# Every SBUF addition and subtraction on VectorE, new durations in the planner, and q/k copies that read runs

## The chip, the cores and the metric

The kernel runs on one core of one Trainium2 chip. The metric is the device time of one launch in microseconds (us), taken as the median of several runs. Five engines work side by side, each through its own list of instructions in order: TensorE (PE, matmuls; PEld is its weight load), VectorE (DVE), ScalarE (ACT), GpSimd (POOL), and SyncE (SP), which here issues all DMAs.

## The reference

Attention with two paths is followed by two feed-forward blocks, all in float32, with batch 4, 8 heads, 576 positions and head dimension 64.

```
# "down" path: q, k, v averaged over 4 neighbours, full softmax attention over 144 positions, repeated 4 times
out_up    = repeat(softmax(q_d @ k_d.T / 8) @ v_d, 4)
# local path: each position sees positions less than 4 away
out_local = softmax(where(|i-j| < 4, q @ k.T / 8, -1e9)) @ v
x = (out_up + out_local) as (2304 tokens, 512)
h = (x @ w1) * (x @ w2) @ w3;  y = h @ w_out            # block A, 1024 wide
z = max(y @ m1, y @ m2, y @ m3);  out = z @ m_out       # block B, 768 wide
```

The feed-forward weights are float64 words in memory and are turned into float32 on the chip.

## The kernel before

**The pieces of work.** `down(b, hp)` does the averaged path for one batch and one pair of heads; there are 16 of them. It loads q and k for the pair as one tile `qk`, copies q and k into position order with two ScalarE copies (L392), folds `qk` twice by additions (L397, L399), makes the scores on PE (L408), the exponentials on ScalarE (L423), scales them (L432), transposes them on PE, folds v twice (L447, L449) and multiplies (L456). `slab(n, ...)` does the local path of 192 tokens of a batch; there are 12. A slab needs the q and k planes and the `down` results of all four head pairs of its batch. Two slabs make the input `xt` of one chunk of 384 tokens.

**The weights.** `weights_product` multiplies w3 by w_out on PE (L591) after `float32` has turned their words into floats: one ScalarE instruction (L358) and four on VectorE (L359, L360, L362, L364) for each tile of 128x1024. The tiles are called `wf`. `pair` does the same for each two blocks of the other weights (tile `cv`) and then splits them: eight pairs for block A, twelve for block B, which can only be loaded into the places that block A has left.

**The split.** All matmuls of the blocks take their operands as a high and a low half: `split` rounds on ScalarE (L334) and subtracts (L336) to get the low half. `mm3` (L341 to L343) is three matmuls for each product. A unit of block A or B is `front` (matmuls `pf`, then `z` by L618 and L620, then a split into `g`) and two units later `back` (matmuls `py`). Block A has 6 chunks of 8 units, block B 6 chunks of 6.

**The order.** Nothing is run in the order in which it is written. `Program.add` notes each task with its engine, its duration in us as a formula of its size, what it reads and what it writes. `Program.order` works out from that a start for each task: `forward` plays the program on a model in which each engine does one task at a time, and takes the ready task with the earliest due time; `backward` works out the due times again; of six rounds the shortest is kept. The engines then run the tasks in exactly that order, whatever the real times are. PE's matmul groups of the blocks are chained in the order of the units; all other tasks move freely.

A task with several options is put by `forward` on the engine that would end it first (L238 to L246). The options are those of `either`: VectorE at 0.18 + 0.00115 us per element, or GpSimd at 0.2 + 0.0024. They are used for L397, L399, L432, L447, L449 and for the subtraction of `split` when its source is in SBUF (L336 for `w`, `xt`, `yt`, `g`). In the trace before, 94 of these run on GpSimd. The model knows of no influence of one engine on another. A task on one engine that feeds another on the same engine counts no delay between them (`lag`); with several options, or from engine to engine, it counts 0.12 to 0.30 us.

Of the kernel before, what the change touches and what calls it, by code (L numbers as in the profile page):

```python
# [15 lines left out]
B, H, S, D = 4, 8, 576, 64  # L16
P = 128
HP = H // 2
NB2 = 2
NR = B // NB2  # L20
NC = 16
TC = S // NC
TT = 12
NJ = TC // TT
NCH = NR * NJ
TG = 4
NG = TT // TG
# [5 lines left out]
GD = S // TG  # L33
# [34 lines left out]
def view(ap, offset, dims):  # L68

    return bass.AP(ap.tensor, ap.offset + offset, [ap.ap[0]] + dims)  # L70
# [202 lines left out]
def attention_moe_kernel(ctx, tc, q0, k0, v0, mask0, ql, kl, vl, mask, qkp, vp, w12, w3t, wo, m123, mo, out):  # L273
# [4 lines left out]
    prog = Program()  # L278
# [23 lines left out]
        return Tile(others, [P, 512], F32, name)  # L302


    act = lambda n: [("ACT", 0.19 + n * 0.00085)]
    dve = lambda n: [("DVE", 0.16 + n * 0.00104)]
    psum = lambda n: [("DVE", 0.15 + n * 0.00104)]
    quick = lambda n: [("DVE", 0.12 + n * 0.0006)]
    either = lambda n: [("DVE", 0.18 + n * 0.00115), ("POOL", 0.2 + n * 0.0024)]
    pe = lambda us: [("PE", us)]  # L310

    def dma(dst, src, reads, writes, size):
# [66 lines left out]
    planes, ods = {}, {}  # L379

    def down(b, hp):
        rd, i = b // NB2, b % NB2 * HP + hp
        qk, k, w = tqr.tile([P, TG * 2 * GD], F32, "qk"), kr.tile([P, KEYS], F32, "k"), qr.tile([P, QUERIES], F32, "q")
        planes[b, hp] = w, k
        dma(lambda: qk(), lambda: qkp[rd, i], [], [qk], P * S * 8)
        v = vrr.tile([KH, 2, 4 * P], F32, "vr")
        dma(lambda: v(), lambda: vp[rd, i].rearrange("r p n -> p r n"), [], [v], KH * 4096 * 2)
        prog.add([("POOL", 0.12)], lambda e: e.memset(k()[:, :W], 0.0), [], [(k, 1)])
        prog.add([("POOL", 0.12)], lambda e: e.memset(k()[:, W + S:], 0.0), [], [(k, 2)])
        prog.add([("POOL", 0.12)], lambda e: e.memset(w()[:, S:], 0.0), [], [(w, 1)])  # L390
        for to, x in ((lambda: w()[:, :S], 0), (lambda: k()[:, W:W + S], GD)):
            prog.add(act(S), lambda e, to=to, x=x: e.copy(  # L392
                to().rearrange("p (c g r) -> p c g r", c=NC, r=TG), view(qk(), x, [[1, NC], [NC, NJ * NG], [2 * GD, TG]])),
                [qk], [(k if x else w, 0)])

        s, vd = qk, vdr.tile([KH, 2, P], F32, "vd")
        prog.add(either(4 * GD), lambda e: e.tensor_tensor(  # L397
            qk()[:, :4 * GD], qk()[:, :4 * GD], qk()[:, 4 * GD:], op=ALU.add), [], [qk])
        prog.add(either(2 * GD), lambda e: e.tensor_tensor(  # L399
            s()[:, :2 * GD], qk()[:, :2 * GD], qk()[:, 2 * GD:4 * GD], op=ALU.add), [], [s])  # L400

        sp = bank("sp")

        def scores(e):
            for w in range(QT):
                for a in range(2):
                    h = slice(a * D, (a + 1) * D)
                    e.matmul(  # L408
                        sp()[h, w * GD:(w + 1) * GD], s()[h, w * QS:w * QS + D], s()[h, GD:2 * GD],
                        start=True, stop=True,  # L410
                    )


        ex = er.tile([P, QT, GD], F32, "e")
        prog.add(pe(0.9), scores, [s], [sp, ex])
        two = twor.tile([P, 2, QT], F32, "two")
        spv = lambda: sp()[:, :QT * GD].rearrange("p (t n) -> p t n", t=QT)
        prog.add(psum(QT * GD), lambda e: e.reduce_max(two()[:, 0], spv(), axis=AX.X), [sp], [two])
        prog.add(act(3), lambda e: e.mul(two()[:, 0], two()[:, 0], -SCALE / 16.0), [], [two])

        def exponentials(e):
            for w in range(QT):
                e.activation(  # L423
                    ex()[:, w, :], spv()[:, w, :], AF.Exp, bias=two()[:, 0, w:w + 1], scale=SCALE / 16.0,
                    accum_out=two()[:, 1, w:w + 1],
                )

        prog.add([("ACT", 1.75)], exponentials, [sp], [ex, two])
        prog.add([("POOL", 0.25)], lambda e: e.tensor_scalar(
            two()[:, 1], two()[:, 1], 4.0, 4e-9, op0=ALU.mult, op1=ALU.add), [], [two])  # L430
        prog.add([("DVE", 0.17)], lambda e: e.reciprocal(two()[:, 1], two()[:, 1]), [], [two])
        prog.add(either(QT * GD), lambda e: e.tensor_tensor(  # L432
            ex(), ex(), view(two(), QT, [[1, QT], [0, GD]]), op=ALU.mult), [two], [ex])
        pt = dpr.tile([KH, 2, 2, QT, QW], F32, "dp")
        for part in range(2):
            pp = bank("pp")

            def transposed(e, part=part, pp=pp):
                for w in range(QT):
                    e.transpose(pp()[:KH, w * P:(w + 1) * P], ex()[:, w, part * KH:(part + 1) * KH], ident)  # L440

            prog.add(pe(0.4), transposed, [ex], [pp, (pt, part)])
            prog.add(act(288), lambda e, part=part, pp=pp: e.copy(
                pt()[:, part].rearrange("p a t n -> p t a n"),
                view(pp()[:KH, :], 0, [[P + QW - QS, QT], [D, 2], [1, QW]]),
            ), [pp], [(pt, part)])
        prog.add(either(4 * P), lambda e: e.tensor_tensor(  # L447
            v()[:, 0], v()[:, 0], v()[:, 1], op=ALU.add), [], [v])
        prog.add(either(2 * P), lambda e: e.tensor_tensor(  # L449
            vd().rearrange("p h n -> p (h n)"), v()[:, 0, :2 * P], v()[:, 0, 2 * P:], op=ALU.add), [v], [vd])  # L450
        po = bank("po")

        def values(e):
            for a in range(2):
                for k in range(2):
                    e.matmul(  # L456
                        po()[a * D:(a + 1) * D, :GD], vd()[:, k, a * D:(a + 1) * D],
                        pt()[:, k, a].rearrange("p t n -> p (t n)"), start=(k == 0), stop=(k == 1),
                    )

        if hp == 0:
            ods[b] = odr.tile([P, HP, GD], F32, "od")
        od = ods[b]
        prog.add(pe(0.7), values, [vd, pt], [po, (od, hp)])
        prog.add(act(GD), lambda e: e.copy(
            od()[:, hp].rearrange("p (c g) -> p c g", c=NC), view(po(), 0, [[1, NC], [NC, NJ * NG]])), [po], [(od, hp)])


    def slab(n, xt, at):
        b, s = divmod(n, NSL)  # L470
# [19 lines left out]
        st = sr.tile([P, 2, 2, HP, BK], F32, "s")  # L490
        sps = [bank("sq") for _ in range(2)]
# [11 lines left out]
                            q[h, t:t + 32], k[h, t:t + BK], start=True, stop=True,  # L503
                        )

        prog.add(pe(2.4), scores, [x for hp in range(HP) for x in planes[b, hp]], [*sps, st])
        for a in range(2):
            prog.add(psum(256), lambda e, a=a: e.tensor_tensor(
                view(st(), a * 256, [[P, 2], [BK, HP], [1, BK]]), view(sps[a](), 0, [[P, 2], [BK, HP], [1, BK]]),
# [53 lines left out]
    def weights_product():  # L563
        raw_places = [place[i] for i in (8, 9, 10, 11, 6, 7)]
        kept = {}

        def plain(at, h, srcs):

            raw = words(raw_places[plain.n % len(raw_places)], srcs, "raw")
            plain.n += 1  # L570
            if h == 0:
                kept[at] = Tile(place[at], [P, 2, 1024], F32, "wf")
            both = kept[at]
            float32(raw, (both, h), lambda: both()[:, h])
            return [((both, h), lambda i=i: both()[:, h, i * 512:(i + 1) * 512]) for i in range(2)]

        plain.n = 0
        wos, w3s = [], [[], []]
        for i in range(NF // 2):
            wos += plain(i // 2, i % 2, [wo[2 * i], wo[2 * i + 1]])  # L580
            w3s[0] += plain(2 + i // 2, i % 2, [w3t[2 * i, :, 0], w3t[2 * i + 1, :, 0]])
        for i in range(NF // 2):
            w3s[1] += plain(4 + i // 2, i % 2, [w3t[2 * i, :, 1], w3t[2 * i + 1, :, 1]])
        for half in range(2):
            os = [Tile(b, [P, 512], F32, "pw") for b in acc]
            for n in range(NF):
                (dw, w), (do, o) = w3s[half][n], wos[n]

                def product(e, n=n, w=w, o=o, os=os):
                    for i in range(4):  # L590
                        e.matmul(os[i](), w()[:, i * P:(i + 1) * P], o(), start=n == 0, stop=n == NF - 1)  # L591

                prog.add(pe(3.5), product, [dw, do], os, chained=True)
            for i in range(4):
                if i % 2 == 0:
                    wp = Tile(place[8 + half * 2 + i // 2], [P, 2, 2, 512], F32R, "wp")
                split(lambda i=i, wp=wp: wp()[:, i % 2, 0], lambda i=i, wp=wp: wp()[:, i % 2, 1], os[i], 512, [os[i]], wp,
                      from_psum=True)
                wa[half * 4 + i, 2] = wp, lambda i=i, wp=wp: wp()[:, i % 2]
# [101 lines left out]
    for n in range(len(units) + LAG):  # L701
# [17 lines left out]
        while gone and gone[0][0] <= n:  # L719
            _, p, f, i = gone.pop(0)  # L720
# [108 lines left out]
```

## Time and profile before

| | |
|---|---|
| median of 3 runs | 828.25 us (823.25 to 828.64) |
| the profiled execution | 827.7 us, span 825.9 us, mean granted PE clock 0.975 |
| PE busy | 771.5 us, 93% of the span |
| DVE busy | 399.7 us, 48% |
| ACT busy | 274.9 us, 33% |
| POOL busy | 138.6 us, 17% |

The span is from the first to the last instruction; the launch adds 1.8 us in the profiled execution. A busy share is a mean over the whole span, so it has to be read for each stretch by itself. A group of instructions is given by its line, engine, operation and tiles, with its busy time and the mean duration of one; where a row gives three durations, they are the shortest, the median and the longest. The granted clock is the share of full speed that TensorE was given: 1.00 is its level of 2.4 GHz, 0.50 its level of 1.2 GHz.

### The profile page before, as it was taken

How to read it: one execution, taken by the hardware profiler on the slowest of the kernel's cores; microseconds unless marked ns; L12 is line 12 of the kernel's file. 1: busy time of each engine (PE TensorE's matmuls, PEld its weight loads, DVE VectorE, ACT ScalarE, POOL GpSimd, SP SyncE). 2: the span in 40 equal slices, each digit the busy share in tenths (PEclk: the TensorE clock that was granted, in tenths of full speed). 3: DMA queues.
4: the chain of work that ended last, by engine and by line, in shares of the span. 5: the costliest groups of instructions: out<-in, count | busy, mean ns of one | idle time of the engine just before them, and what ended most of it. 6: DMA issues, size and time to landing. Idle time of an engine off the chain costs nothing.

```text
span 825.9 us, 16670 instructions
## 1 busy us (share of the span) xinstructions
PE 771.5 (93%) x7120; PEld 711.2 (86%) x7120; DVE 399.7 (48%) x614; ACT 274.9 (33%) x585; POOL 138.6 (17%) x176
## 2 busy tenths in 40 slices
PE   2879877998999999999998999999999999999997
PEld 0334446998999989999998999899999999999997
DVE  5978999924143274254324599972222131311211
ACT  4255574331234443363212355422121121121111
POOL 2213479500001012010001026520000000000000
PEclk9999976999999999999999999999999999999999
DMA  9786553012103232221202377112101001010001
GB/s 336 230 309 202 160 176 77 15 49 60 39 4 77 67 103 56 77 72 26 60 6 89 121 240 252 61 44 87 39 1 39 1 1 39 1 39 0 20 20 39
DMA packets 45482, 68.85 MB, mean 83 GB/s; under 512 B 20640, under 2 KB 29856, under 8 KB 45408
## 3 DMA queue, kind: packets, MB, share of 16 engines
q1 hardware_dynamic: 45408, 67.79, 25.7%
q8 instruction: 56, 0.92, 0.5%
q14 instruction: 18, 0.15, 0.1%
HBM read 58.33 MB, written 9.44 MB: 82 GB/s over the span
## 4 chain that ended last, share of the span: by engine, by line
PE 75%; DVE 11%; DMA 7%; issue 4%; ACT 1%; POOL 1%; SPq 1%; ACTq 0%; POOLq 0%; DVEq 0%
PE pf L341 16%; PE pf L343 15%; PE pf L342 15%; PE py L341 7%; PE py L342 6%; PE py L343 6%; PE poq L543 3%; DVE cv L362 3%; DMA qk<-qkp 2%; PE pw L591 2%; DVE cv L364 2%; DMA vr<-vp 2%; PE sq L501 1%; DVE cv L360 1%; PE sp L408 1%
## 5 line engine op out<-in xcount | busy, mean ns | idle before, releaser
L620 DVE TENSOR_TENSOR z<-pf,z 128x384 f32<-128x384 f32 x120 | 66.7, 556 | 287.5 <-PE pf L343 287.2
L341 PE MATMUL pf<-yt,w 128*128 128x384 f32 x432 | 146.0, 338 | 1.4 <-DVE z L620 1.4
L343 PE MATMUL pf<-yt,w 128*128 128x384 f32 x432 | 145.9, 338 | 0.0
L342 PE MATMUL pf<-yt,w 128*128 128x384 f32 x432 | 145.9, 338 | 0.0
L341 PE MATMUL pf<-xt,w 128*128 128x384 f32 x384 | 134.3, 350 | 1.9 <-issue 1.1
L342 PE MATMUL pf<-xt,w 128*128 128x384 f32 x384 | 132.0, 344 | 2.1 <-POOL xt L336 2.1
L343 PE MATMUL pf<-xt,w 128*128 128x384 f32 x384 | 131.6, 343 | 0.0
L618 ACT COPY z<-pf 128x384 f32<-128x384 f32 x84 | 40.2, 479 | 168.2 <-PE pf L343 168.2
L334 ACT CAST g<-z 128x384 fp32r<-128x384 f32 x84 | 43.1, 513 | 149.4 <-DVE z L620 149.3
L591 PE MATMUL pw<-wf 128*128 128x512 f32 x128 | 66.1, 669 | 24.9 <-DVE wf L364 22.6
L341 PEld LDWEIGHTS pf<-yt,w 128*128 128x128 f32 x432 | 81.1, 188 | 2.0 <-issue 1.7
L342 PEld LDWEIGHTS pf<-yt,w 128*128 128x128 f32 x432 | 81.1, 188 | 0.0
L343 PEld LDWEIGHTS pf<-yt,w 128*128 128x128 f32 x432 | 81.1, 188 | 0.0
L341 PEld LDWEIGHTS pf<-xt,w 128*128 128x128 f32 x384 | 73.9, 192 | 4.7 <-issue 2.7
L591 PEld LDWEIGHTS pw<-wf 128*128 128x128 f32 x128 | 26.6, 216 | 57.8 <-issue 32.4
L342 PEld LDWEIGHTS pf<-xt,w 128*128 128x128 f32 x384 | 73.8, 192 | 2.6 <-POOL xt L336 2.6
L343 PEld LDWEIGHTS pf<-xt,w 128*128 128x128 f32 x384 | 73.7, 192 | 0.0
L341 PE MATMUL py<-g,wp 128*128 128x384 f32 x192 | 67.1, 350 | 0.4 <-ACT o L649 0.4
L342 PE MATMUL py<-g,wp 128*128 128x384 f32 x192 | 64.8, 338 | 2.1 <-issue 2.1
L343 PE MATMUL py<-g,wp 128*128 128x384 f32 x192 | 64.9, 338 | 0.0
L336 DVE TENSOR_TENSOR g<-z,g 128x384 fp32r<-128x384 f32 x72 | 42.2, 587 | 33.3 <-ACT g L334 33.0
L341 PE MATMUL py<-g,w 128*128 128x384 f32 x144 | 48.9, 340 | 1.9 <-ACT o L649 1.9
(90 smaller groups left out, 1118.2 us busy)
## 6 DMA issues: line engine op xcount, KB each, us to landing
qk<-qkp SPq DMA_DIRECT2D x16, 576.0 KB
raw<-m SPq DMA_DIRECT2D x18, 512.0 KB
raw<-w3t SPq DMA_DIRECT2D x16, 512.0 KB
raw<-w SPq DMA_DIRECT2D x16, 512.0 KB
vr<-vp SPq DMA_DIRECT2D x16, 288.0 KB
y_dram<-o SPq DMA_DIRECT2D x48, 96.0 KB
y<-y_dram SPq DMA_DIRECT2D x16, 288.0 KB
out<-o SPq DMA_DIRECT2D x24, 192.0 KB
```

What stands on the lines that cost most here:

```text
L334: prog.add(act(n), lambda e: e.copy(hi(), src()), reads, [(writes, ("hi", id(hi)))])
L336: psum(n) if from_psum else either(n), lambda e: e.tensor_tensor(lo(), src(), hi().bitcast(F32), op=ALU.subtract),
L341: nc.tensor.matmul(o, wlo, xhi, start=first, stop=False)
L342: nc.tensor.matmul(o, whi, xlo, start=False, stop=False)
L343: nc.tensor.matmul(o, whi, xhi, start=False, stop=last)
L360: prog.add(quick(1024), lambda e: e.tensor_scalar(u(), u(), 3, 0x3FFFFFF8, op0=ALU.logical_shift_left, op1=ALU.bitwise_and), [], [cv])
L362: prog.add(dve(1024), lambda e: e.scalar_tensor_tensor(u(), high(), 0xC0000000, u(), op0=ALU.bitwise_and, op1=ALU.bitwise_or), [raw], [cv])
L364: prog.add(dve(1024), lambda e: e.scalar_tensor_tensor(u(), low(), 29, u(), op0=ALU.logical_shift_right, op1=ALU.bitwise_or), [raw], [cv])
L543: e.matmul(pos[u]()[a * D:(a + 1) * D, i * BQ:(i + 1) * BQ], vw()[h, a, i], pt().rearrange("p a n -> p (a n)")[h, c:c + BQ], start=True, s ...
L591: e.matmul(os[i](), w()[:, i * P:(i + 1) * P], o(), start=n == 0, stop=n == NF - 1)
L618: prog.add(act(T), lambda e, pp=pp: e.copy(z(), pp()[:, :T]), [pp], [z])
L620: prog.add(psum(T), lambda e, pp=pp: e.tensor_tensor(z(), pp()[:, :T], z(), op=ALU.mult if kind == "A" else ALU.max), [pp], [z])
```

## The change

The option of GpSimd is gone: `either` is now the same formula as `dve`, so all its users run on VectorE, and their tasks have one option. The formulas of ScalarE, of `quick` and `psum`, and four durations of PE groups are replaced. The two copies of L392 do the same reordering with the loops in another order: before, the innermost loop read elements 288 apart and wrote neighbours; now it reads runs of 16 neighbours (144 of them in a row) and writes elements 36 apart; their planned duration is 1.0 us. What is computed is the same. Since the planner works from the durations, the order on every engine is worked out anew.

```
-    act = lambda n: [("ACT", 0.19 + n * 0.00085)]
+    act = lambda n: [("ACT", 0.14 + n * 0.00098)]
     dve = lambda n: [("DVE", 0.16 + n * 0.00104)]
-    psum = lambda n: [("DVE", 0.15 + n * 0.00104)]
-    quick = lambda n: [("DVE", 0.12 + n * 0.0006)]
-    either = lambda n: [("DVE", 0.18 + n * 0.00115), ("POOL", 0.2 + n * 0.0024)]
+    psum = dve
+    quick = lambda n: [("DVE", 0.16 + n * 0.00052)]
+    either = dve
...
         for to, x in ((lambda: w()[:, :S], 0), (lambda: k()[:, W:W + S], GD)):
-            prog.add(act(S), lambda e, to=to, x=x: e.copy(
-                to().rearrange("p (c g r) -> p c g r", c=NC, r=TG), view(qk(), x, [[1, NC], [NC, NJ * NG], [2 * GD, TG]])),
+            prog.add([("ACT", 1.0)], lambda e, to=to, x=x: e.copy(
+                to().rearrange("p (c g r) -> p r g c", c=NC, r=TG),
+                qk().rearrange("p (r x g c) -> p r x g c", r=TG, x=2, c=NC)[:, :, x // GD]),
                 [qk], [(k if x else w, 0)])
...
-        prog.add(pe(0.9), scores, [s], [sp, ex])
+        prog.add(pe(0.95), scores, [s], [sp, ex])
...
-            prog.add(pe(0.4), transposed, [ex], [pp, (pt, part)])
+            prog.add(pe(0.45), transposed, [ex], [pp, (pt, part)])
...
-        prog.add(pe(0.7), values, [vd, pt], [po, (od, hp)])
+        prog.add(pe(1.05), values, [vd, pt], [po, (od, hp)])
...
-        prog.add(pe(2.4), scores, [x for hp in range(HP) for x in planes[b, hp]], [*sps, st])
+        prog.add(pe(1.55), scores, [x for hp in range(HP) for x in planes[b, hp]], [*sps, st])
...
-                prog.add(pe(3.5), product, [dw, do], os, chained=True)
+                prog.add(pe(3.45), product, [dw, do], os, chained=True)
```

## Rows read from the trace of the kernel before

**Rows 1.** The page: busy time of each engine over the whole span

```profile
PE 771.5 (93%) x7120; PEld 711.2 (86%) x7120; DVE 399.7 (48%) x614; ACT 274.9 (33%) x585; POOL 138.6 (17%) x176
```

**Rows 2.** Busy time by stretch: length, then each engine's busy us, PE clock, DMA

```profile
8.00:162.00 154.00, 121.97 (x1216) 77.54 (x1217) 140.85 (x164) 77.85 (x146) 73.49 (x65) 0.89 0.58 190
162.00:450.00 288.00, 281.98 (x3710) 268.26 (x3709) 111.63 (x228) 98.03 (x230) 23.11 (x49) 0.99 0.20 56
450.00:550.00 100.00, 96.30 (x657) 94.51 (x656) 82.65 (x96) 46.23 (x87) 35.56 (x25) 1.00 0.45 149
```

**Rows 3.** What PE waited for: us in total, times, longest

```profile
PE pw L591 <- DVE wf L364: 22.6, 3, 16.2
```

**Rows 4.** Busy time by stretch, two stretches at the low clock

```profile
105.00:111.80 6.80, 5.64 (x17) 3.13 (x18) 6.70 (x10) 3.46 (x11) 3.13 (x3) 0.50 0.45 133
122.00:139.10 17.10, 10.38 (x215) 9.14 (x212) 16.93 (x18) 10.21 (x22) 15.94 (x11) 0.50 0.40 100
```

**Rows 5.** Groups on POOL from 8 to 162 us: busy us, mean ns, idle before

```profile
L336 POOL TENSOR_TENSOR w<-cv,w 128x512 fp32r<-128x512 f32 x9 | 15.9, 1774 | 1.8 <-ACT w L334 1.0 <-DVE two L431 0.7
L447 POOL TENSOR_TENSOR vr<-vr 72x512 f32<-72x512 f32 x8 | 12.5, 1568 | 6.7 <-DVE cv L360 3.7 <-DMA vr<-vp 2.8
L397 POOL TENSOR_TENSOR qk<-qk 128x576 f32<-128x576 f32 x7 | 11.5, 1649 | 16.1 <-ACT k L392 16.1
L449 POOL TENSOR_TENSOR vd<-vr 72x256 f32<-72x256 f32 x6 | 8.4, 1395 | 1.3 <-DVE two L431 1.0
L399 POOL TENSOR_TENSOR qk<-qk 128x288 f32<-128x288 f32 x6 | 7.7, 1288 | 7.0 <-issue 6.8
L336 POOL TENSOR_TENSOR xt<-x,xt 128x384 fp32r<-128x384 f32 x4 | 5.9, 1473 | 0.6 <-ACT xt L334 0.6
L336 POOL TENSOR_TENSOR g<-z,g 128x384 fp32r<-128x384 f32 x3 | 4.5, 1502 | 4.5 <-ACT g L334 4.5
...
L432 POOL TENSOR_TENSOR e<-e,two 128x432 f32<-128x432 f32 x3 | 3.0, 1003 | 5.3 <-DVE two L431 5.3
```

**Rows 6.** Line 336 over the whole span: shortest, median, longest ns

```profile
L336 DVE TENSOR_TENSOR g<-z,g x72: 545/559/1841, 163.3 to 816.1; 128x384 fp32r<-128x384 f32 x72
...
L336 DVE TENSOR_TENSOR w<-cv,w x20: 675/684/3122, 93.9 to 550.2; 128x512 fp32r<-128x512 f32 x20
...
L336 DVE TENSOR_TENSOR wp<-pw,wp x8: 673/673/676, 60.3 to 121.7; 128x512 fp32r<-128x512 f32 x8
```

**Rows 7.** The instructions of tile cv: shortest, median, longest ns

```profile
L334 ACT CAST w<-cv x40: 610/618/642, 92.9 to 549.5; 128x512 fp32r<-128x512 f32 x40
...
L359 DVE TENSOR_SCALAR cv<-cv x20: 679/686/3173, 81.4 to 544.6; 128x1024 f32<-128x1024 f32 x20
L360 DVE TENSOR_SCALAR cv<-cv x20: 686/1246/1976, 82.1 to 545.7; 128x1024 uint32<-128x1024 uint32 x20
L362 DVE SCALAR_TENSOR_TENSOR cv<-raw,cv x20: 1207/1796/2326, 88.1 to 546.4; 128x1024 uint32<-128x1024 uint32 x20
L364 DVE SCALAR_TENSOR_TENSOR cv<-raw,cv x20: 1207/1226/2226, 91.6 to 547.7; 128x1024 uint32<-128x1024 uint32 x20
```

**Rows 8.** Tile cv's instructions alone, from 8 and from 450 us: DVE, ACT, POOL busy

```profile
8.00:162.00 154.00, 53.19 (x39) 18.73 (x24) 15.89 (x9) 0.89 0.58 190
450.00:550.00 100.00, 66.44 (x60) 27.52 (x36) 19.12 (x11) 1.00 0.45 149
```

**Rows 9.** Tile wf's instructions alone, from 8 us: PE, PEld, DVE, ACT busy

```profile
8.00:162.00 154.00, 66.08 (x128) 26.61 (x128) 50.84 (x48) 12.93 (x12) 0.89 0.58 190
```

**Rows 10.** Line 392, the q copies: shortest, median, longest ns

```profile
L392 ACT COPY q<-qk x16: 1207/1230/1281, 16.6 to 359.7; 128x576 f32<-128x576 f32 x16
```

**Rows 11.** What DVE waited for: us in total, times, longest

```profile
DVE qk L397 <- ACT k L392: 11.4, 6, 4.6
...
DVE vr L447 <- DMA vr<-vp: 4.7, 4, 2.1
```

## The prediction

> **What bounds the kernel now.** The page comes first: PE is busy for 93% of the span, DVE for 48%, POOL for 17% [rows 1]. By that mean the change would touch nothing. So the second view is busy time by stretch [rows 2]. From 8 to 162 us DVE is busy for 140.85 of 154 us, and PE for 121.97. From 162 to 450 us it is the other way round: PE 281.98 of 288, DVE 111.63. From 450 to 550 us, where block B's weights are converted, DVE has 82.65 of 100 and PE still 96.30. So the kernel has two regimes: DVE sets the pace up to about 162 us, after that PE does, and DVE comes near only once more. Third come the waits of PE: the longest kind is for the last conversion step on DVE, 22.6 us in three waits, of which one is the 16.2 us until the first weights are there [rows 3]. Fourth, the granted clock: in 105 to 111.8 and in 122 to 139.1 us it is 0.50, the 1.2 GHz level, and PE is busy there for 5.64 and 10.38 us [rows 4]; it has idle time in both, and DVE is busy for 6.70 of 6.80 and 16.93 of 17.10. So what can be won up to 162 us is bounded: PE idles 154 - 121.97 = 32.0 us, of which 16.2 - 8 = 8.2 wait for the first weights and stay; 23.8 us are left, and at most half of 5.64 + 10.38, 8.0 us, are lost to the clock.
>
> **Part 1, what goes to DVE.** From 8 to 162 us POOL does 46 additions and subtractions in 15.9 + 12.5 + 11.5 + 8.4 + 7.7 + 5.9 + 4.5 + 3.0 = 69.4 us [rows 5]. On DVE, undisturbed, the subtraction takes 559 ns for 384 elements and 684 for 512 [rows 6]: 0.98 ns an element and 184 ns fixed. By these two rows I estimate 747 ns for 576 elements, 606 for 432, 465 for 288, 434 for 256 (those on 72 partitions too). Added to DVE: 9 x 0.684 + 8 x 0.684 + 7 x 0.747 + 6 x 0.434 + 6 x 0.465 + 4 x 0.559 + 3 x 0.559 + 3 x 0.606 = 28.0 us.
>
> **Part 2, what DVE gets back.** The conversions show what POOL costs DVE. Their four steps take 679, 686, 1207 and 1207 ns at their shortest, 3.78 us together, but have longest values of 1976 to 3173 [rows 7], and the same split on DVE goes from 675 to 3122 ns [rows 6]. From 8 to 162 us tile cv has 39 instructions on DVE in 53.19 us [rows 8]: eight conversions at 3.78 and seven splits at 0.675 would be 35.0, so 18.2 us are lost. Tile wf: 48 instructions in 50.84 us [rows 9], twelve conversions would be 45.4, so 5.5 are lost (11%). The rest of DVE's work there, 140.85 - 53.19 - 50.84 = 36.8 us, has lost between nothing and cv's share (34%, 12.6 us); I take wf's share, 4.0, because much of it reads PSUM, and the subtraction from PSUM never takes over 676 ns [rows 6]. Back: 27.7 us. The net is +0.3 us of DVE work, between 28.0 - 23.7 = +4.3 and 28.0 - 36.3 = -8.3. I take 0.
>
> The Trainium skill (SBUF — State Buffer, section "SBUF: two separate sides") says that VectorE and GpSimd share one pair of ports under an exclusive lock, so that the loser waits for the whole instruction. By that alone, up to the whole 69.4 us of POOL's instructions could stand against DVE, and taking them away would give back up to 41 us net; the rows on the conversions show a loss of 23.7, so the sum goes by those.
>
> From 450 to 550 us cv's 60 instructions took 66.44 us [rows 8]; undisturbed, 12 x 3.78 + 12 x 0.675 = 53.5. So 13.0 come back. Moved are POOL's 25 instructions [rows 2]: eleven of cv's splits, 7.5 us, and fourteen of at most 0.559 each, 7.8. The net is at most +2.3 us, and PE has only 3.7 us of idle time there to win; I take -1.5. From 162 to 450 us POOL is busy for 23.11 us, which is less than half of that on DVE; DVE has 176 us free there, so I cost it at nothing. If that cover failed, the whole move of some 10 us would be its price.
>
> **Part 3, the order.** The old model books a conversion's third step at 0.16 + 1024 x 0.00104 = 1.22 us whatever POOL does, while its median was 1.80 [rows 7]; it books a 512-element subtraction on POOL at 1.43 us, while it took 1.77 [rows 5]; and a q or k copy at 0.68, while it took 1.23 [rows 10]. So the lists fixed for 8 to 162 us come from a model in which POOL is free help. Seven first folds of the averaged path are on POOL alone by then [rows 5], though the first chunk needs four; the model put the others in as cover. With one option each, the new model's DVE durations are what an undisturbed DVE shows (0.69 for 512 elements, 1.22 for 1024), and a crowded DVE is visible to the planner. Two gains follow. First, DVE idles 154 - 140.85 = 13.1 us in this stretch; I take 40% of it, 5 us. The bounds are nothing and 13. Second, four averaged paths of the second batch (each some 0.75 + 0.47 + 0.68 + 0.43 + 0.61 = 2.9 us of the moved kinds, 11.8 together) can run behind more urgent conversions; as they are still needed before the second chunk I take a quarter, 3 us, between 0 and 11.8. PE's own durations change by at most 0.85 us a group; that gives other interleavings, at no price that I can sign.
>
> **Part 4, the copies.** Nothing in the trace shows the new form. A contiguous cast of 512 elements takes 618 ns [rows 7], so 576 would be about 0.70; the old form takes 1.23 [rows 10]. The writes are now 36 elements apart, and no row excludes that they are slower than the old reads; as far again to the other side would be 1.76. I take the middle of the first two, 0.96: 32 x 0.27 = 8.6 us less on ACT, which is busy for 77.85 of 154 us [rows 2], so it is hidden except where DVE waits for it: 11.4 us in six waits at the first fold [rows 11]. Few of these lie where DVE sets the pace; I take -0.5. At 1.76 the cover is ACT's other half, and the price would be about +0.5 for each late fold.
>
> **The sum.** The profiled execution took 827.7 us (span 825.9), 0.55 under the median of 828.25. 0 - 1.5 - 5 - 3 - 0.5 = -10, so 817.7: **818 us**, with a range of its own from 810 to 822.
>
> **The rivals.**
>
> *A wash.* DVE's load is what sets the pace up to 162 us, and it stays the same; the planner finds nothing better, since the 13.1 us of idle time are waits for loads and for PE's scores. For it: parts 1 and 2 cancel. Against it: PE idles 23.8 us there beyond its start, at half the clock for part of it. Time: 827.7 + 0.3 - 1.5 to + 4.3, so 824 to 832.
>
> *DVE's queue blocks (slower).* Each moved instruction waits in DVE's list where POOL did the waiting, and the conversions behind it wait too; PE waits for these. The place is the first folds of q/k and v up to 162 us: seven and eight are moved [rows 5]. On DVE the nine first folds waited 11.4 us for ACT's copies, 1.27 each, and the seven v folds 4.7 us for their load, 0.67 each [rows 11] (each line has 16 over the span, of which DVE had nine and seven). 7 x 1.27 + 8 x 0.67 = 14.3 us, which in this stretch all reach the end: 827.7 + 0.3 + 14.3 - 1.5 = 841 at the worst, 837 with a fourth of it won back by order. It decides from about 10 us of such waits. Against it: those waits lie mostly where DVE has time, and the planner knows of the loads. The Trainium skill (Perfetto Trace Analysis, "Optimizing Scalar/DVE Operations") speaks for this rival: where DVE is saturated, it says, giving work to other engines, even GpSimd, may make sense; it adds that the shared port may make that useless, and the longest values of the conversions fit the second half.
>
> *More than forecast.* The planner, seeing true costs, brings the first chunk's units forward by most of what is open: 13.1 us of DVE's idle time plus half of the 11.8 us of deferred folds, -1.5 and -0.5: 827.7 - 21 = 807. The same time would come if the unshown 36.8 us of DVE had lost cv's share.
>
> **Chances.** Forecast 0.42 (four fifths of it below 820), more than forecast 0.14, wash 0.31, slower 0.13. A measurement of this kernel can tell about 1%, 8.3 us, from no change. Faster by more: 0.14 + 0.34 = 0.48; within: 0.08 + 0.29 = 0.37; slower: 0.13 + 0.02 = 0.15. The range that holds 8 in 10 runs from 804 (the far end of the third rival) to 833 (past the wash), and leaves out most of the slower case.
>
> **What would show it.** On the changed kernel's page POOL should have some 82 instructions left (176 - 94) and a few us. The conversion steps should stand at their shortest, 0.68, 0.69, 1.21 and 1.21 us, everywhere; if longest values of 2 us remain, part 2 is wrong. DVE's busy time over the span should stay within some 10 us of 399.7 although it has 94 instructions more. PE's idle time from 8 to 162 us should fall from 32.0 to about 24, with less time at 0.50; if it stays, part 3 is wrong and the wash has come. If waits of DVE at L397 and L447 reach 10 us before 162 us, the slower rival has. The copies should take 0.7 to 1.23 us; 1.5 or more would make part 4 wrong.

## The result and the profile after

The changed kernel takes 804.47 us (800.37 to 806.03) against 827.21 us for the kernel before: a ratio of 0.9725, 95% interval 0.9672 to 0.9778. That is 22.7 us less. The forecast was 818 us, 10 us less; its own range from 810 to 822 was missed, and the wide range from 804 to 833 holds the time only at its very end. The profiled executions are 803.13 and 827.7 us.

The page's busy line of the changed kernel, to be held against [rows 1]:

```profile
PE 764.2 (95%) x7120; PEld 707.8 (88%) x7120; DVE 395.3 (49%) x708; ACT 274.3 (34%) x585; POOL 12.2 (2%) x82
```

POOL has lost its 94 instructions, DVE has 94 more and yet 4.4 us less busy time. Then busy time by stretch, as in [rows 2]:

```profile
8.00:162.00 154.00, 135.76 (x1470) 93.08 (x1471) 144.03 (x227) 84.86 (x168) 5.73 (x20) 0.97 0.58 194
162.00:450.00 288.00, 282.62 (x3688) 269.58 (x3687) 118.05 (x252) 97.89 (x228) 2.79 (x29) 0.98 0.21 59
450.00:550.00 100.00, 99.12 (x564) 98.80 (x563) 78.33 (x119) 44.58 (x83) 0.00 (x0) 1.00 0.45 152
```

PE's idle time from 8 to 162 us is 18.2 us instead of 32.0, at a mean clock of 0.97 instead of 0.89. But equal times are not equal work: PE started 1216 matmul instructions in that stretch before and 1470 after. A better cut is the moment when the first unit of the second chunk of block A starts (its first matmul of L343). In the kernel before that is at 196.6 us, in the changed one at 173.9. The next two fences have the stretch up to this cut and the one behind it, first before, then after:

```profile
8.00:196.60 188.60, 154.22 (x1770) 107.39 (x1771) 153.96 (x192) 88.41 (x174) 75.70 (x68) 0.91 0.51 166
...
196.60:825.90 629.30, 617.28 (x5352) 603.84 (x5350) 245.75 (x423) 184.33 (x410) 59.20 (x75) 0.99 0.18 57
```

```profile
8.00:173.90 165.90, 146.40 (x1770) 102.59 (x1771) 148.28 (x238) 87.95 (x174) 5.73 (x20) 0.97 0.57 186
...
173.90:801.40 627.50, 617.78 (x5352) 605.21 (x5350) 246.97 (x471) 184.17 (x410) 2.79 (x29) 0.99 0.18 57
```

Up to the cut PE has started 1770 matmul instructions in both, so the two stretches can be compared: 188.6 - 165.9 = 22.7 us of the difference lie here, 1.8 behind it. PE's idle time goes from 34.4 to 19.5, 14.9 us less, and the same matmuls take 146.40 instead of 154.22 us of busy time, 7.8 less, at a mean clock of 0.97 instead of 0.91. That is the whole 22.7. (The medians are 22.7 us apart too, which is chance: the spans of the two profiled executions are 24.5 apart.) The clock is large enough to carry the 7.8: up to the cut PE is busy at the 1.2 GHz level for 26.2 us before, in five stretches that start at 36.7, 50.3, 70.8, 105 and 122 us, and for 8.2 us after, in two that start at 44.6 and 102.6 us; half of the difference is 9.0.

The conversions of tile cv (shortest, median, longest ns, as in [rows 7]) are undisturbed everywhere:

```profile
L336 DVE TENSOR_TENSOR w<-cv,w x40: 679/686/693, 83.6 to 524.0; 128x512 fp32r<-128x512 f32 x40
...
L359 DVE TENSOR_SCALAR cv<-cv x20: 683/686/695, 72.5 to 517.4; 128x1024 f32<-128x1024 f32 x20
L360 DVE TENSOR_SCALAR cv<-cv x20: 682/690/695, 74.2 to 519.2; 128x1024 uint32<-128x1024 uint32 x20
L362 DVE SCALAR_TENSOR_TENSOR cv<-raw,cv x20: 1209/1224/1229, 75.3 to 519.9; 128x1024 uint32<-128x1024 uint32 x20
L364 DVE SCALAR_TENSOR_TENSOR cv<-raw,cv x20: 1161/1225/1227, 76.6 to 521.2; 128x1024 uint32<-128x1024 uint32 x20
```

The copies, against [rows 10], have become slower, not faster:

```profile
L392 ACT COPY q<-qk x16: 1225/1265/1312, 21.4 to 336.1; 128x576 f32<-128x576 f32 x16
L392 ACT COPY k<-qk x16: 1260/1290/1321, 22.5 to 337.1; 128x576 f32<-128x576 f32 x16
```

And DVE's waits, against [rows 11]: the seven first folds of q and k and the nine of v that came over, counted over the whole span, have not made them longer.

```profile
DVE vr L448 <- DMA vr<-vp: 4.1, 3, 3.0
...
DVE qk L398 <- ACT k L392: 2.5, 5, 0.7
```

### The profile page after: what moved, and what is told of

It is laid out like the page before. It is cut to its first block, busy times and chain, and to the rows that moved or that the text cites. A ratio compares the mean times of both kernels' runs of the same rounds, so it can differ in the third digit from the quotient of the medians.

```text
span 801.4 us, 16601 instructions
## 1 busy us (share of the span) xinstructions
PE 764.2 (95%) x7120; PEld 707.8 (88%) x7120; DVE 395.3 (49%) x708; ACT 274.3 (34%) x585; POOL 12.2 (2%) x82
## 4 chain that ended last, share of the span: by engine, by line
PE 90%; DVE 4%; DMA 2%; issue 2%; ACT 1%; SPq 0%; ACTq 0%
PE pf L341 18%; PE pf L342 18%; PE pf L343 18%; PE py L341 8%; PE py L342 7%; PE py L343 7%; PE pw L592 6%; PE poq L544 3%; PE sq L502 2%; PE sp L409 2%; PE pp L441 1%; PE po L457 1%; PE ptq L527 1%; DMA y_dram<-o 1%; DMA raw<-wo 1%
## 5 line engine op out<-in xcount | busy, mean ns | idle before, releaser
L343 PE MATMUL pf<-yt,w 128*128 128x384 f32 x432 | 145.9, 338 | 0.0
L343 PE MATMUL pf<-xt,w 128*128 128x384 f32 x384 | 131.2, 342 | 0.0
L592 PE MATMUL pw<-wf 128*128 128x512 f32 x128 | 61.9, 638 | 20.2 <-DVE wf L364 20.2
L343 PEld LDWEIGHTS pf<-yt,w 128*128 128x128 f32 x432 | 81.1, 188 | 0.0
L343 PEld LDWEIGHTS pf<-xt,w 128*128 128x128 f32 x384 | 73.3, 191 | 0.6 <-issue 0.6
L343 PE MATMUL py<-g,wp 128*128 128x384 f32 x192 | 65.1, 339 | 0.0
L336 DVE TENSOR_TENSOR g<-z,g 128x384 fp32r<-128x384 f32 x84 | 46.7, 556 | 34.8 <-ACT g L334 34.7
```

The lines of the kernel that those rows point to most:

```text
L336: psum(n) if from_psum else either(n), lambda e: e.tensor_tensor(lo(), src(), hi().bitcast(F32), op=ALU.subtract),
L343: nc.tensor.matmul(o, whi, xhi, start=False, stop=last)
```

## The experiments

All ratios are to the kernel before, run on the same chip, with 95% intervals. The planner makes lists, and the lists then run somewhere; the first two kernels take these apart.

**e1: old lists, all on VectorE.** The planner is the old one; where it chose GpSimd, VectorE runs the task.

```
     order = prog.order()
+    order = [(t, "DVE" if len(t.options) > 1 else e) for t, e in order]
```

> The old planner with its two options and old durations fixes the lists; the 94 tasks that it gave to GpSimd then run on VectorE at the same places of the order. Theory order (the gain comes from the new lists, the move itself is a wash): DVE's work from 8 to 162 us changes by +0.3 us, the first unit of block A still starts near 131.9 us, total 820 to 832 us. Rival placement (the gain comes from VectorE being undisturbed): first unit near 105 us, total 803 to 812 us.

Measured: 813.66 us, 0.9869 (0.9835 to 0.9903), between the two expected ranges; its first unit started at 123.0 us, near neither of the expected times. The move alone, with no new order, is worth 1.3%. The same cut, the start of the second chunk, shows where it comes from. First the stretch to the second chunk, then tile cv and tile wf alone in it (DVE is the third column of the first and of wf's row, the first of cv's):

```profile
8.00:184.90 176.90, 151.94 (x1770) 107.38 (x1771) 147.10 (x238) 88.62 (x174) 3.64 (x20) 0.91 0.53 176
...
8.00:184.90 176.90, 40.50 (x48) 18.57 (x24) 0.91 0.53 176
...
8.00:184.90 176.90, 62.08 (x128) 24.92 (x128) 45.30 (x48) 12.86 (x12) 0.91 0.53 176
```

With 46 instructions more, DVE is busy for 147.10 us instead of 153.96. Tile cv, with nine splits more, takes 40.50 instead of 53.19, tile wf 45.30 instead of 50.84. All else on DVE has 37 instructions more and takes 61.3 instead of 49.9. PE's idle time falls by 34.4 - 25.0 = 9.4 us, its busy time by 2.3. A rival is that PE simply no longer waits for GpSimd's slower steps. Before, PE's waits that end with GpSimd are 2.7 us up to the cut, and e1 has none, so waits of this direct kind are the smaller part; how much longer chains of steps add was not tried.

**e2: new lists, the old 94 tasks on GpSimd.**

```
     order = prog.order()
+    on_pool = {...}     # the numbers of the 94 tasks
+    order = [(t, "POOL" if t.n in on_pool else e) for t, e in order]
```

> The changed kernel's order, but the same 94 tasks that ran on GpSimd before run there again. Theory order: most of the gain stays, first unit of block A near 105 us, the longer steps of GpSimd cost some 5 us, total 804 to 814 us. Rival placement: the conversions are slowed again by some 24 us up to 162 us and 13 us from 450 us, total 820 to 830 us.

Measured: 810.98 us, 0.9827 (0.9793 to 0.986). The time is in the range of the theory order. The lists alone are worth 1.7%, though the conversions are disturbed again:

```profile
L360 DVE TENSOR_SCALAR cv<-cv x20: 679/694/1784, 75.3 to 529.4; 128x1024 uint32<-128x1024 uint32 x20
L362 DVE SCALAR_TENSOR_TENSOR cv<-raw,cv x20: 1215/1263/2336, 76.4 to 530.5; 128x1024 uint32<-128x1024 uint32 x20
```

They are disturbed less than in the kernel before, where the medians were 1246 and 1796 [rows 7], and up to the second chunk (at 181.9 us) tile cv takes 47.82 us on DVE instead of 53.19. So part of what the new lists give is that the two engines get in each other's way less often. 1.3% and 1.7% make 3.0%, the two together 2.75%: within the intervals they add up, but they are not wholly separate causes.

**e3 and e14: only the option gone; e4 and e13: only the durations.** e3 is the kernel before with

```
-    either = lambda n: [("DVE", 0.18 + n * 0.00115), ("POOL", 0.2 + n * 0.0024)]
+    either = lambda n: [("DVE", 0.18 + n * 0.00115)]
```

and e4 the changed kernel with the option back and the old copies:

```
-    either = dve
+    either = lambda n: [*dve(n), ("POOL", 0.2 + n * 0.0024)]
```

e14 and e13 are the same two with VectorE's fixed parts 0.01 us higher, so that the planner comes to another plan.

> The kernel before with the GpSimd option taken out of either (VectorE at 0.18 + 0.00115 us per element, as before) and nothing else. Theory order, first form (the planner only has to see that VectorE is crowded): second batch's folds are put off, first unit near 103 us, total 800 to 810 us. Second form (the corrected durations are needed too): 812 to 822 us. Rival placement: 803 to 810 us as well, so only a time above 812 speaks.

> As e3 (old durations, option gone), with VectorE's fixed parts 0.01 us higher. If taking the option out is what makes the gain: 798 to 812 us. If e3 was lucky and the durations are needed: above 814 us.

> The changed kernel's durations, but the GpSimd option kept (VectorE by the new formula, GpSimd at 0.2 + 0.0024) and the old form of the q and k copies. Theory order, first form: the planner still counts on GpSimd as free help, first unit near 130 us, total 820 to 830 us. If the durations alone make the good order: first unit near 105 us, total 803 to 814 us. Rival placement: 820 to 830 us, VectorE's conversions with longest values of 2 us.

> As e4 (new durations, GpSimd option kept, old copies), with VectorE's fixed part 0.01 us higher. If the new durations make a better plan even with GpSimd in it: 806 to 818 us again. If e4 was a lucky plan: 820 to 832 us, like the old durations' plans.

Measured: the option gone gives 806.75 us, 0.9777 (0.9751 to 0.9803), and 810.13 us, 0.979 (0.9757 to 0.9823). The durations alone give 812.08 us, 0.984 (0.9808 to 0.9872), and 815.85 us, 0.9858 (0.983 to 0.9887). So each edit of the model makes a faster kernel by itself, on two plans. e4 still ran 81 tasks on GpSimd; its first unit started at 116.6 us, near neither of the expected times. In e3 and e14 the move to VectorE is contained: against the old lists run on VectorE (e1, and e16 below) they are 0.9% and 0.5% faster, which is hardly more than the 0.6% by which plans differ by chance. Taking the option out also changes the planned delay between two tasks on VectorE (`lag`) to nothing; this part was not tried alone.

**e12, e16, e8, e15, e9: how much a plan moves by chance.** e12 is the kernel before, e8 and e15 the changed kernel, each with VectorE's fixed part moved by 0.01 us; e16 is e12's lists run wholly on VectorE; e9 plans VectorE with a fixed part of 0.06.

```
-    dve = lambda n: [("DVE", 0.16 + n * 0.00104)]
+    dve = lambda n: [("DVE", 0.17 + n * 0.00104)]     # e8, e12 (there psum and either too); e15 0.15; e9 0.06, quick too
```

> The kernel before with the fixed part of VectorE's three formulas 0.01 us higher: how much the old planner's result moves by chance. If the old plan was a typical one: 820 to 832 us. If it was an unlucky one: 805 to 818 us, and part of the gain of the new order would be luck.

> e12's lists (old durations nudged, planned with GpSimd, 831.7 us) with all of GpSimd's additions and subtractions run on VectorE, as e1 did with the lists of before. If the placement is worth about 1.3% whatever the plan: 817 to 824 us. If e1 was one lucky pairing: 826 to 833 us.

> The changed kernel with the fixed part of VectorE's planned duration at 0.17 instead of 0.16 us: a control for how much a plan differs by chance. If the order's gain is a property of the model: within 1% of the changed kernel, 798 to 812 us. If it is a lucky plan: 812 to 825 us.

> The changed kernel with VectorE's fixed part 0.01 us lower, the other side of e8. If plans of this kind scatter by chance within some 1.5%: 797 to 810 us. A time outside would show that the scatter is wider than e7, e8 and e9 let expect.

> The changed kernel with VectorE planned by the distance from start to start instead of by the recorded duration: in the trace two back-to-back 512-element subtractions start 0.60 us apart though each is recorded with 0.69, and 1024-element steps 1.14 apart with 1.22; the fixed part of the formulas goes from 0.16 to 0.06. If the model's accuracy on VectorE matters: 795 to 803 us. If the plan is good enough already: 800 to 808 us.

Measured: e12 831.73 us, 1.0067 (1.0042 to 1.0092); e16 812.31 us, 0.9839 (0.9792 to 0.9886); e8 798.78 us, 0.9663 (0.9643 to 0.9682); e15 799.95 us, 0.9676 (0.964 to 0.9711); e9 805.55 us, 0.9742 (0.9715 to 0.9769). A nudge that means nothing moves the ratio of either kernel by some 0.6% (for the changed kernel the intervals overlap), and e8, the fastest of all runs, is ahead of the changed kernel by no more than that. e16 came out below both of its expected ranges. Planning with the distance from start to start (e9) brought nothing beyond that. From e12 to e16 the placement is worth more than in e1, 2.3% (1.0067 to 0.9839), on a plan that is worse to begin with.

| lists planned | additions run on | ratios |
|---|---|---|
| with GpSimd, old durations | GpSimd | 1, 1.0067 |
| with GpSimd, new durations | GpSimd | 0.984, 0.9858 |
| with GpSimd, old durations | VectorE | 0.9869, 0.9839 |
| the changed kernel's | GpSimd | 0.9827 |
| without GpSimd, old durations | VectorE | 0.9777, 0.979 |
| without GpSimd, new durations (the last two with further ones, e9 and e7) | VectorE | 0.9725, 0.9663, 0.9676, 0.9742, 0.9813 |

**e6, e10 and e11: do the second batch's folds matter?** Each adds a condition for the planner alone. In the kernel before, the second batch's first folds also read the first weight pair (e6) or the first chunk's input (e10); in the changed kernel, the first unit also reads the folded q, k and v (e11).

```
+        later = [wa[0, 0][0]] if b == 1 else []      # e6;  e10: [xs["A", 0]]
...
+            early = folded if (kind, ch, f) == ("A", 0, 0) else []      # e11
-            prog.add(pe(12 * MM), products, [dw, xt], [pp], chained=True)
+            prog.add(pe(12 * MM), products, [dw, xt, *early], [pp], chained=True)
```

> The kernel before, GpSimd option and old durations kept; for the planner alone the first folds of q/k and v of the second batch also need the first converted weight pair of block A. Theory deferral (the new lists gain because the second batch's folds no longer stand ahead of the first unit): first unit near 105 to 115 us instead of 131.9, total 810 to 818 us. Rival (the gain of the lists is spread over many small waits): first unit a little earlier, total 820 to 828 us.

> The kernel before (GpSimd option, old durations); for the planner alone the first folds of the second batch also need the first chunk's finished input, so three of the four cannot stand ahead of the first unit (the condition of e6, the first weight pair, was met too early, and its folds stayed ahead). Theory deferral: first unit near 112 to 122 us, total 810 to 820 us. If putting off is worth nothing by itself: first unit near 127 us and total 822 to 832 us.

> The changed kernel; for the planner alone the first unit of block A also needs the second batch's folds of q, k and v, which puts these ahead of it as in the kernel before. Everything runs on VectorE undisturbed and the durations are the new ones. Theory deferral: first unit at 115 to 123 us, total 810 to 816 us, as with the old lists on VectorE (813.7 us). Rival (spread over many small waits): 802 to 808 us.

Measured: e6 831.99 us, 1.0062 (1.0035 to 1.0088), outside both expected ranges; its first unit still started at 127.5 us, since its condition was met too early. e10 819.16 us, 0.9921 (0.9893 to 0.995): its first unit started at 113.0 us, and both this and the time are where the theory of deferral expected them. But 0.8% is little more than the 0.6% that a nudge moves, so e10 neither shows that putting off helps the kernel before nor excludes it. e11 804.35 us, 0.9735 (0.9702 to 0.9768), the same as the changed kernel. The start of block A (first of the two start times) in the kernel before, in the changed one, and in e11:

```profile
L343 PE MATMUL pf<-xt,w x384: 331/337/525, 131.9 to 506.4; 128*128 128x384 f32 x192
```

```profile
L343 PE MATMUL pf<-xt,w x384: 331/337/522, 102.7 to 486.2; 128*128 128x384 f32 x192
```

```profile
L343 PE MATMUL pf<-xt,w x384: 332/337/522, 122.4 to 487.4; 128*128 128x384 f32 x192
```

The change brought the first unit forward by 29.2 us, the most striking difference of the two traces; e11 gives 19.7 of that back and loses nothing. When its second chunk starts, at 178.7 us and so 4.8 us later than in the changed kernel, PE has started 128 matmul instructions more; I read this as work done early that is not in the way later. In the changed kernel the early first unit is not the cause of the gain.

**e5 and e7: the copies, and more durations.** e5 is the changed kernel with the old form of L392 at the same planned duration. e7 adds five durations.

```
-            prog.add([("ACT", 1.0)], ...      # e5: the old view() form at 1.0
+            prog.add([("ACT", 1.12)], ...     # e7, the old form too; local scores 1.25, local products 1.0,
+                                              #     last product of down 0.65, exponentials 1.2
```

> The changed kernel with the q and k copies in their old form (planned at 1.0 us as in the changed kernel, so that the lists stay the same). The trace after shows the new copies at 1.27 and 1.29 us, the old ones took 1.23. If the copies matter: a few us slower. If not, as the copies' trace says: 802 to 808 us, the same as the changed kernel or up to 1 us faster.

> The changed kernel with the old, 0.04 us shorter form of the copies and five more durations as the traces show them (copies by their distance 1.12, averaged path's last product 0.65, local scores 1.25, local products 1.0, exponentials 1.2 us). If a truer model gives a better order: 794 to 801 us. If plans at this level differ by chance only: 798 to 808 us.

Measured: e5 804.75 us, 0.972 (0.9689 to 0.975), no difference. e7 809.9 us, 0.9813 (0.9771 to 0.9856): the plan with five more durations nearer to the traces is 0.9% slower than the changed kernel's, outside both expected ranges.

## Why the forecast was too small

**What bounds the kernel** was right as to the place: 22.7 of the 24.5 us between the spans come from the stretch to the second chunk, and DVE is busy for 148.28 of 165.9 us there. The bound on the clock was wrong: 8.0 us is half of PE's busy time in two stretches at 0.50, but there are three more, at 36.7, 50.3 and 70.8 us, and half of all five is 13.1.

**Parts 1 and 2, the placement, were mis-sized.** I took 0; e1 has 11.7 us less to the second chunk. The losses of cv and wf were right: undisturbed I had 35.0 + 6.2 for cv with its nine new splits and 45.4 for wf, against 40.50 and 45.30. What failed is the rest: 21.8 us for the other 37 tasks less 4.0, so +17.8, while e1 shows +11.4. The rows by line divide these 6.4 us. Count times mean, added up over the rest's lines, is 57.1 us before and 73.2 in e1, so +16.1: the moved tasks cost 21.6, as forecast, but the rest had lost 5.5 us, measured against its means in e1, and not 4.0. The largest part of it is L432, whose mean was 995 ns before, on five instructions, and is 602 in e1 (count, busy us, mean ns):

```profile
L432 DVE TENSOR_TENSOR e<-e,two 128x432 f32<-128x432 f32 x5 | 5.0, 995 | 0.0
...
L432 DVE TENSOR_TENSOR e<-e,two 128x432 f32<-128x432 f32 x8 | 4.8, 602 | 0.0
```

The other 4.7 us are overlap. Busy time counts a moment once, and I priced every moved task at its recorded duration. Back to back on DVE they cost less, as the changed kernel's timeline shows (start, us, what):

```profile
83.04 0.68 DVE L359 TENSOR_SCALAR cv<-cv 128x1024 f32<-128x1024 f32 x1
83.64 0.68 DVE L336 TENSOR_TENSOR w<-cv,w 128x512 fp32r<-128x512 f32 x1
...
86.66 0.69 DVE L360 TENSOR_SCALAR cv<-cv 128x1024 uint32<-128x1024 uint32 x1
87.38 1.23 DVE L362 SCALAR_TENSOR_TENSOR cv<-raw,cv 128x1024 uint32<-128x1024 uint32 x1
```

The first two are recorded with 0.68 us and start 0.60 apart, an overlap of 0.08. L362, which reads what L360 has just written, starts 0.72 after it and does not overlap. A task put between two such steps overlaps with both neighbours: in e1, L362 starts at 100.29 us and takes 1.22, L449 starts at 101.43 and takes 0.42, and L364 starts at 101.76. So I estimate a saving of 0.08 to 0.16 us for each moved task; 4.7 us over 37 tasks is 0.13. The Trainium skill (Perfetto Trace Analysis, "Optimizing Scalar/DVE Operations") says that VectorE has an overhead of some 60 ns for an instruction on SBUF, and that the profiled latency holds about twice this, since the half that acknowledges the write overlaps with the next instruction; the 0.08 us here are of that size. The remaining 4.8 us of e1 are idle time of DVE that went (34.6 to 29.8 us), which I had booked under the order.

The lock rule of the Trainium skill (SBUF — State Buffer, "SBUF: two separate sides") by itself allowed up to 41 us; DVE's work to the second chunk fell by 6.9 in e1. The direction agrees, the full size does not.

**Part 3, the order, was mis-sized, and its second gain was wrong.** I took 5 + 3; the changed lists give 14.3 us by e2's ratio, or 184.9 - 173.9 = 11.0 to the second chunk on top of e1. Of these 11.0, 151.94 - 146.40 = 5.5 are the clock: the same 1770 matmul instructions, at a mean of 0.97 instead of 0.91. The sum has no term for the clock at all; 7.8 us came back by it from the kernel before to the changed one. The 3 us for deferred folds were for a mechanism that e11 shows to be worth nothing in the new model; for the old one e10 leaves open some 7 us, of which a nudge alone can make 5.5. The 29 us of the first unit, too, would have been read as its proof without that run.

That a planner without the option of GpSimd makes better lists is borne out only weakly (e3 and e14 against e1 and e16, 0.9% and 0.5%). That I gave the new durations of other steps "no price that I can sign" was too little: with GpSimd still an option they give 1.6% and 1.4% on two plans (e4, e13), more than a nudge. Without it they give 0.5 to 1.3% in the changed kernel and its nudges, but e7, with still more of them, is 0.4% behind e3: a warning against any single plan. Which of the durations does it was not tried; on PE the change replaces five planned durations, not four as said above.

**Part 4, the copies,** was wrong in sign and without weight: 1.27 and 1.29 instead of 1.23 us, inside the bounds 0.70 and 1.76, not the 0.96 that I took.

**450 to 550 us** came out near: PE's idle time there went from 3.7 to 0.9, and the stretch behind the second chunk is 1.8 us shorter, against the 1.5 taken. In e1 that stretch is 626.2 us, 3.1 shorter than before, so plans differ there by as much, and the agreement is partly luck.

**The slower rival** did not come: up to 162 us DVE waits for 0.2 us at the first folds of q and k and not at all at those of v; the wait of 3.0 us shown above lies behind that. The rival took its price from waits of which, in the kernel before, only 0.6 us lay in this stretch. **The wash** fell with e1; its lower end of 824 does not come out of its sum, which gives 826.5. **More than forecast** is where the time lies, 804 against 807, by a path of its own, and so by luck: the time came from the placement and from the clock, not from folds put off, and the rest of DVE's work had lost 5.5 us, not cv's share of 12.6.

## What to carry to other kernels

Work moved to a saturated engine is to be priced at the distance from start to start among instructions that do not wait for each other, not at its recorded duration, and what it disturbed is to be taken off. Cut two traces of a two-regime kernel at equal work, not at equal times: idle time and time lost to the clock then add up to the whole difference. Where a planner writes the order, nudge a number that means nothing before crediting an edit of under 1%, and force the striking difference alone before calling it the cause.

## What was not expected of the hardware

On ScalarE the copy of 576 elements costs much the same whether the reads are 288 apart and the writes in a row (1.23 us) or the reads in runs and the writes 36 apart (1.27 and 1.29), about twice a contiguous cast of 512 (0.62). On VectorE two instructions recorded with 0.68 us start 0.60 us apart, but 0.72 when the second reads what the first wrote. And PE's mean clock from 8 us to the second chunk was 0.91 with idle time of 34.4 us and 0.97 with 19.5: beside the 14.9 us of idle time 7.8 us came back through the clock. The sum of the gaps does not settle the clock, though: in e1, with 25.0 us of idle time, it was still 0.91.
